# Attention, ELU feed-forward and routed experts in one kernel: a tile's scores beside its neighbour's values, independent table scatters, early expert count from 14 tiles

## Chip, core and metric

The kernel runs on one core of a Trainium2 chip. The metric is the device time of one execution in microseconds (us). Engines are named as the profile names them: PE is TensorE (PEld its weight loads), DVE is VectorE, ACT is ScalarE, POOL is GpSimd, SP is SyncE, which issues most DMAs. Each engine works through its own instructions strictly in the order in which they stand, and waits on semaphores.

## What is computed

Three stages follow each other, on 4 x 576 = 2,304 tokens of width 512 (8 heads of 64):

```python
# 1. attention, causal, window of 64 tokens, float32
scores = where(0 <= pos_i - pos_j < 64, q @ k.T / 8, -1e9)
x = softmax(scores) @ v                      # (2304, 512)
# 2. feed-forward, weights float64: w_in (512, 2048), w_out (2048, 512)
h = x @ w_in
y = where(h > 0, h, exp(min(h, 0)) - 1) @ w_out
# 3. one expert of 8 per token, w1 (8, 512, 1024), w2 (8, 1024, 512)
logits = y @ w_gate + modality_bias[modality_id]     # modality_id is 0 or 1
e = argmax(logits);  gate = softmax(logits)[e]
out = gate * (relu(y @ w1[e]) @ w2[e])
```

With the reference's inputs the bias decides: all tokens fall to two experts, one for each modality.

## The kernel before

**Tiles and units.** The tokens are 18 tiles of 128, or 9 groups of 256. Attention goes by units: unit n = 2t + qd is four heads (qd) of tile t. Each unit is a chain of pieces: `ld`/`lv` load k, q and v (SP); `1p` transposes k and q (PE, 4 matmuls, `p_t`), `1e` copies them out of PSUM; `2p` makes the scores (`p_s`: contraction over 64, output over 64 rows, so the array is split in 64x64 tiles); `2d` adds the mask and takes the maximum (DVE), `2x` the exponential (ACT), `2n` the reciprocal (DVE), `2m` the normalisation (POOL); `3p` transposes the weights (PE, `p_a`), `3a` copies them (`PA`); `4p` multiplies by v (`p_o`: the array split in 128x64 tiles); `4a` and `4d` copy the result as a high and a low part (`xh`, `xl`).

**Feed-forward.** Every product is three float32r products of high and low parts. `f1(g,s)` is 24 matmuls of 256 columns for group g and 256 of the 2,048 inner columns (`h`), `f2(g,s)` 12 matmuls of 512 columns into `y`. Between them stand ACT (`fx`, `fe`, `fh`), DVE (`fm`) and, for the low part, POOL (`fl`, L571) or DVE. The float64 weights are turned into two float32r halves in 32 half-tiles during groups 0 and 1 (`wa` ACT, `wb` DVE, `wc`, `wd`: `wd` on DVE or POOL by the table `LE`).

**Routing.** After a group's `y` the gate takes 8 dot products per tile (`g1`, DVE), the choice (`g2d`), a rank by a matmul with a triangle (`g3p`, PE, `p_rk`; `g3d`, DVE), and `g3s` (POOL, L650), an indirect DMA that writes each token's row of a table `tab` in DRAM, sorted by expert. After 16 of the 18 tiles a first count (`ep` PE, `ed` DVE) finds the expert that has the most tokens, so that its weights can be loaded (`el`, SP) and its first three stages (EA = 3) of 256 tokens can begin: `xa` (SP) reads the table, `xb` (POOL, L879) gathers the rows of y, `xp` transposes them, `e1`/`e2` are the products with 24 and 12 matmuls each. The final count (`rp`, `rd`, `r2`) sets the stages 3 to 8.

**What sets the order.** `program()` lists the pieces with an engine, a cost, a rank, the pieces they need and the buffers they take and free. `plan()` goes through time with these costs and writes each engine's order; the kernel is built in that order. Tables of numbers (ranks such as `G1R`, `RDR`, and ranges such as `LE`, `VIA`, `E1D`, which say on which engine a copy runs) steer it. Up to a planned time of 40 us, PE's planned waits are filled with matmuls on the identity (`fill`).

Of the kernel before, what the change touches and what calls it, by code (L numbers as in the profile page):

```python
# [81 lines left out]
def fused(ctx, tc, q, k, v, w_in, w_out, mod, w_gate, mbias, w1, w2, out):  # L82
# [11 lines left out]
    EA = 3  # L94
# [7 lines left out]
    G1R = 91.22  # L102
    RDR = -290.43
    R2R = -989.45
    EXR = -764.4
    XDR = -890.0
    XBL = 6.4
    SGL = 16.34
    SG = 13.52
    FG = 0.3  # L110
    LV = -17.16
    UR = (0.85, 2.04)
    HE = range(28, 32)
    LE = range(0, 15)
    VIA = range(0, 19)
    E1D = range(0, 6)
    A3D = range(0, 1)
    A4D = range(0, 0)
    FXA = (0, 1, 2, 3, 4, 5, 6, 7, 8)
    YX = (1, 2, 6, 7)  # L120
    LG = 19.41
# [25 lines left out]
    ptp = mkpool("pt", 1)  # L147
# [12 lines left out]
    masks = const.tile([128, 3, 2, 128], F32, name="masks")  # L160
# [72 lines left out]
    def load_gate():  # L233
        cut, fill, zero = RT["sg"]
        wg = cut(128, 4, E)
        nc.sync.dma_start(out=wg, in_=w_gate.rearrange("(k p) e -> p k e", p=128))
        RT["wg"] = wg
        bb = cut(128, 2, E)
        nc.sync.dma_start(out=bb, in_=mbias.partition_broadcast(128))
        md = cut(NTILE, 128, 2, dt=I32)  # L240
        nc.sync.dma_start(out=md, in_=mod.bitcast(I32).rearrange("(t p two) -> t p two", p=128, two=2))
        RT["sg"] = cut, bb, md
        nc.sync.dma_start(out=tab.rearrange("(p r) c -> p r c", p=128), in_=fill)
        for r0, n in ((NT - 256, 128), (NT - 128, 128), (NT, 1)):
            nc.sync.dma_start(out=yd[r0:r0 + n, :].rearrange("p (a b) -> p a b", b=64),
                              in_=zero[0:n].rearrange("p (o b) -> p o b", o=1).to_broadcast([n, DM // 64, 64]))
# [116 lines left out]
    def a2p(t, qd):  # L363
        u = U[t, qd]
        p = u["p2"] = [ps.tile([128, 2, 128], F32, tag="ps", name="p_s") for _ in range(2)]
        for i in range(2):
            for b, r in enumerate(HALF):
                for z in range(2):
                    mm(p[z][r, i], KQ[qd][HALF[z], 2 + i, t % 2, r], window(t, qd, z, i, b), start=True, stop=True)
# [42 lines left out]
    def a4p(t, qd):  # L412
        u = U[t, qd]
        PA, va = u.pop("PA"), u.pop("v")
        po = u["p4"] = ps.tile([128, 2, 128], F32, tag="ps", name="p_o")
        for h in range(4):
            i, z = divmod(h, 2)
            for r, b in zip(HALF, range(2)):
                mm(po[HALF[z], i, r], va[:, b, h], PA[:, h, r], start=True, stop=True)

    def x_at(t, qd):
        return (a[:, 2 * qd:2 * qd + 2, 128 * (t % 2):128 * (t % 2) + 128] for a in X[t // 2])

    def a4a(t, qd, eng):
        if t // 2 not in X:
            new_x(t // 2)
        xh, xl = x_at(t, qd)
        put(eng, xh, U[t, qd]["p4"])

    def a4d(t, qd):  # L430
        po = U.pop((t, qd))["p4"]
        xh, xl = x_at(t, qd)
        dve.tensor_tensor(out=xl, in0=po, in1=xh, op=ALU.subtract)  # L433
# [214 lines left out]
    def g3s(t):  # L648
        GT.pop(t)
        pool.indirect_dma_start(out=tab[:, :], out_offset=bass.IndirectOffsetOnAxis(ap=FI.pop(t)[:, 0:1], axis=0),  # L650
                                in_=ent[:, t, :], in_offset=None)
# [17 lines left out]
    def early_p():  # L669
        p = RT["p0"] = ps.tile([1, E], F32, tag="ps", name="p_c0")  # L670
        mm(p, ones[:, 0:1], cnt[NTILE - 3], start=True, stop=True)

    def early_d():
# [13 lines left out]
        e0, b0 = f0[:, 0:1], f0[:, 1:2]  # L687
        lt = sm("lt0", EA - 1)
        for s in range(1, EA):
            dve.tensor_scalar(out=lt[:, s - 1:s], in0=m0[:, 0:1], scalar1=256.0 * (s + 1), scalar2=None, op0=ALU.is_lt)  # L690
# [4 lines left out]
        for s in range(1, EA):  # L695
# [3 lines left out]
            dve.scalar_tensor_tensor(out=b, in0=gap, scalar=lt[:, s - 1:s], in1=b, op0=ALU.mult, op1=ALU.add)  # L699
# [312 lines left out]
    def program():  # L1012
# [6 lines left out]

        units = [(t, qd) for t in range(NTILE) for qd in range(2)]  # L1020
        for n, u in enumerate(units):
            t, qd = u
            back = t > 0
            early = n < NEARLY
            r = n * UR[0] if n < 8 else 8 * UR[0] + (n - 8) * UR[1]
            add(("ld", n), "SP", 2.9 if n == 0 else KQC * len(list(runs(128 * t, 128))), u_kq, *u, rank=n - 20, need={"w": 1} if early else {"ld": 1},
                lat=1.1 if early else 2.4)
            add(("lv", n), "SP", 0.61 * v_loads(t), u_v, *u, rank=n + LV, deps=[("ld", n)], need={} if early else {"v": 1},
                lat=1.0 if early else 2.4)
            w2p = [("2p", n - 2)] if back else []  # L1030
# [16 lines left out]
            add(("4p", n), "PE", 0.78, a4p, *u, rank=r - 1000, deps=[("3a", n), ("lv", n)] + ([("4p", n - 1)] if n % 4 else []),
                need={"ps": 1} if n % 4 else {"ps": 1, "X": 1},
                free={"PA": 1} | ({"w": 1} if early else {"v": 1}), lat=0.25)
            add(("4a", n), e4, 0.29 if e4 == "ACT" else 0.34, a4a, *u, e4, rank=r,  # L1050
                deps=[("4p", n)] + ([("4a", n - 1)] if n % 4 else []))
            add(("4d", n), "DVE", 0.34, a4d, *u, rank=r, deps=[("4a", n)], free={"ps": 1})
# [18 lines left out]
        for g in range(NG):  # L1071
            for s in range(NP):
# [6 lines left out]
                    deps=[("wd", "i", s, 0), ("wd", "i", s, 1)] + [("4d", 4 * g + x) for x in range(4)] + ([("f1", g, s - 1)] if s else [("f1", g - 1 - (g < NG - 1), NP - 1)] if g > 1 else []),  # L1079
# [18 lines left out]
        add(("sg", 0), "SP", 4.0, load_gate, rank=SG - 20, deps=[("sg", 5)], lat=2.5)  # L1098
# [6 lines left out]
        for t in range(NTILE):  # L1105
# [21 lines left out]
        for j in range(8):  # L1127
            add(("el", j), "SP", 1.8, lambda j=j: e_load(RT["v0"], j), rank=j - 600.0, deps=["ed"] + [("xa", s) for s in range(EA)],
# [3 lines left out]
        for s in range(NS):  # L1132
# [42 lines left out]
        caps = {"w": 33, "ps": 4, "h": 2, "y": 1, "P": 2, "v": 3, "ld": 2, "PA": 1, "X": 3, "e": 2, "g": 3,  # L1175
# [56 lines left out]
```

## Time and profile before

| | |
|---|---|
| median of 3 runs | 760.13 us (759.86 to 760.77) |
| profiled execution | 758.43 us, of which the span from first to last instruction is 756.5 us |
| PE busy | 734.6 us, 97% of the span |
| DVE, ACT, POOL busy | 57%, 44%, 27% |
| granted TensorE clock, mean | 0.993 |

A matmul's row shows its whole passage through the array, and matmuls overlap, so a busy PE says little. What a matmul costs is read from the distance of its start to the start of the next one: the timeline (start, duration, engine, line, operation) has both. A row with a releaser in square brackets was preceded by idle time that this releaser ended. [...]

### The profile page before, as it was taken

The page shows a single profiled execution, that of the slowest core. Times are in us where ns is not written, and L with a number is a line of the kernel's source. Part 1 is how long each engine was busy: PE and PEld are TensorE (multiplying, and loading weights), DVE is VectorE, ACT ScalarE, POOL GpSimd, SP SyncE. Part 2 cuts the span into 40 slices and gives each one's busy share as a digit, 9 for nine tenths or more (in the row PEclk, how much of TensorE's full clock was granted, in tenths as well). Part 3 has the DMA queues.
Part 4 walks back from the last instruction along what each step waited for, and adds up shares of the span by engine and source line. Part 5 has one row for each costly group of instructions (what it writes and reads, how often), then busy time and mean ns, then how long its engine had stood idle before and what let it go on. Part 6 is the DMA issues. An engine that isn't in the chain of part 4 may idle for free. (4 is left out here: it accounts for less than half of the span.)

```text
span 756.5 us, 14736 instructions
## 1 busy us (share of the span) xinstructions
PE 734.6 (97%) x5534; PEld 651.0 (86%) x5534; DVE 430.1 (57%) x1311; ACT 332.6 (44%) x799; POOL 201.0 (27%) x192
## 2 busy tenths in 40 slices
PE   8999999999998999999999999998999999999996
PEld 7878988888886988888988989986988999989995
DVE  6999996899393158194186183584983124421210
ACT  5987854674553463455346333334421114311211
POOL 5201434134223223224224223234024112111011
PEclk9999999999999999999999999999999999999999
DMA  8999532431321031220020000007218212000001
GB/s 204 242 238 294 228 119 113 129 81 30 78 56 41 4 98 29 57 72 22 18 75 1 1 29 1 29 1 254 81 29 293 81 46 72 17 29 14 15 29 43
DMA packets 101020, 62.26 MB, mean 82 GB/s; under 512 B 83697, under 2 KB 87939, under 8 KB 100811
## 3 DMA queue, kind: packets, MB, share of 16 engines
q1 hardware_dynamic: 97323, 51.51, 24.2%
q0 software_dynamic: 3616, 9.72, 3.8%
q8 instruction: 45, 0.74, 0.5%
q14 instruction: 36, 0.29, 0.2%
HBM read 51.05 MB, written 10.42 MB: 81 GB/s over the span
## 5 line engine op out<-in xcount | busy, mean ns | idle before, releaser
L515 PE MATMUL h<-xh,whi 128*128 128x256 f32 x576 | 166.2, 289 | 2.4 <-DVE e L560 2.0
L516 PE MATMUL h<-xl,whi 128*128 128x256 f32 x576 | 163.0, 283 | 0.3 <-DVE xl L433 0.3
L517 PE MATMUL h<-xh,wlo 128*128 128x256 f32 x576 | 162.9, 283 | 0.0
L571 POOL TENSOR_TENSOR g<-e,g 128x512 fp32r<-128x512 f32 x53 | 71.5, 1350 | 183.7 <-ACT g L564 183.5
L524 PE MATMUL y<-whi,g 128*128 128x512 f32 x288 | 118.0, 410 | 0.0
L526 PE MATMUL y<-whi,g 128*128 128x512 f32 x288 | 114.2, 396 | 2.5 <-POOL g L571 2.2
L515 PEld LDWEIGHTS h<-xh,whi 128*128 128x128 f32 x576 | 110.1, 191 | 5.6 <-DVE e L560 2.4
L525 PE MATMUL y<-wlo,g 128*128 128x512 f32 x288 | 113.7, 395 | 0.0
L516 PEld LDWEIGHTS h<-xl,whi 128*128 128x128 f32 x576 | 110.3, 191 | 1.7 <-DVE xl L433 0.5
L517 PEld LDWEIGHTS h<-xh,wlo 128*128 128x128 f32 x576 | 110.1, 191 | 0.0
L560 DVE SCALAR_TENSOR_TENSOR e<-e,h 128x512 f32<-128x512 f32 x53 | 36.3, 685 | 101.0 <-ACT e L551 85.4
L545 ACT ACTIVATE e<-h 128x512 f32<-128x512 f32 x72 | 42.8, 594 | 115.8 <-PE h L517 112.9
L515 PE MATMUL h<-xh,ehi 128*128 128x256 f32 x256 | 72.6, 284 | 0.0
L516 PE MATMUL h<-xl,ehi 128*128 128x256 f32 x256 | 72.5, 283 | 0.0
L517 PE MATMUL h<-xh,elo 128*128 128x256 f32 x256 | 72.5, 283 | 0.0
L526 PEld LDWEIGHTS y<-whi,g 128*128 128x128 f32 x288 | 54.5, 189 | 17.1 <-POOL g L571 2.6
L938 DVE SCALAR_TENSOR_TENSOR g<-h,g 128x512 fp32r<-128x512 f32 x32 | 22.0, 689 | 79.5 <-ACT g L933 79.4
L933 ACT ACTIVATE g<-h 128x512 fp32r<-128x512 f32 x32 | 19.1, 596 | 106.1 <-PE h L517 98.7
L524 PEld LDWEIGHTS y<-whi,g 128*128 128x128 f32 x288 | 54.8, 190 | 12.3 <-issue 2.4
L386 ACT ACTIVATE sm<-sm,st 128x128 f32<-128x128 f32 x144 | 56.0, 392 | 19.6 <-DVE st L379 19.5
L525 PEld LDWEIGHTS y<-wlo,g 128*128 128x128 f32 x288 | 54.9, 191 | 9.2
L601 DVE CUSTOM_DVE_ANT_0 lgs<-ysb,wgb 128x512 bf16<-128x512 f32 x80 | 61.4, 768 | 1.9
(214 smaller groups left out, 1437.8 us busy)
## 6 DMA issues: line engine op xcount, KB each, us to landing
raw<-in_moe_w_in_dram SPq DMA_DIRECT2D x16, 512.0 KB, 5.1
raw<-in_moe_w_out_dram SPq DMA_DIRECT2D x16, 512.0 KB, 5.8
wraw<-in_moe_w_dram SPq DMA_DIRECT2D x16, 512.0 KB, 11.7
v<-in_v_dram SPq DMA_DIRECT2D x46, 128.0 KB, 2.9
kq<-in_k_dram SPq DMA_DIRECT2D x30, 128.0 KB, 2.7
kq<-in_q_dram SPq DMA_DIRECT2D x30, 128.0 KB, 3.0
v<-in_v_dram SPq DMA_DIRECT2D x44, 64.0 KB, 3.0
yd<-ysb SPq DMA_DIRECT2D x10, 256.0 KB, 2.7
```

The lines of the kernel that those rows point to most:

```text
L386: act(out=sm[:, h], in_=sm[:, h], func=AF.Exp, bias=st[:, 0, h:h + 1], scale=-1.0, accum_out=st[:, 1, h:h + 1])
L515: mm(hs[c], w[0][:, d, f], xh, start=d == 0, stop=False)
L516: mm(hs[c], w[0][:, d, f], xl, start=False, stop=False)
L517: mm(hs[c], w[1][:, d, f], xh, start=False, stop=d == 3)
L524: mm(y, gh[:, m], w[0][:, c], start=first and c == 0, stop=False)
L525: mm(y, gh[:, m], w[1][:, c], start=False, stop=False)
L526: mm(y, gl[:, m], w[0][:, c], start=False, stop=last and c == 1)
L545: act(out=e, in_=H[g, s], func=AF.Relu, scale=-1.0)
L560: dve.scalar_tensor_tensor(out=h if via_psum(g, s) else e, in0=e, scalar=-1.0, in1=h, op0=ALU.add, op1=ALU.max)
L571: pool.tensor_tensor(out=a[:, 1], in0=e, in1=a[:, 0], op=ALU.subtract)
L601: dve.tensor_tensor_reduce(out=lgs, in0=y, in1=wgb[:, e], scale=1.0, scalar=0.0, op0=ALU.mult, op1=ALU.add, accum_out=GT[t][:, e:e + 1])
L938: dve.scalar_tensor_tensor(out=g[1][:, c], in0=h, scalar=0.0, in1=g[0][:, c], op0=ALU.max, op1=ALU.subtract)
```

## The change

Four things change. From tile 6 on the two units of a tile are taken together: `24` is one PE piece that makes the values of tile t-1 (both units, one PSUM tile) and then the scores of tile t (both units, two PSUM tiles). It has two `PA` buffers where there was one; the mask is bfloat16; `4a` and `4d` handle both units at once. The table scatters are declared independent of each other. The first count is taken after 14 tiles in place of 16 (`EC`); stage 0 too is now dropped if the largest expert has too few tokens, two more tiles of `yd` are zeroed at the start, and the first three gathers need groups up to 6 alone. The tables and some costs have other numbers, so that all orders differ.

```diff
-    EA = 3
+    EA, EC = 3, NTILE - 4
-    LE = range(0, 15)
-    VIA = range(0, 19)
+    LE = range(0, 27)
+    VIA = range(0, 15)
...
-    ptp = mkpool("pt", 1)
+    ptp = mkpool("pt", 2)
-    masks = const.tile([128, 3, 2, 128], F32, name="masks")
+    masks = const.tile([128, 3, 2, 128], BF16, name="masks")
-        for r0, n in ((NT - 256, 128), (NT - 128, 128), (NT, 1)):
+        for r0, n in [(128 * t, 128) for t in range(EC, NTILE)] + [(NT, 1)]:
...
+    def a2p(t, *qds):
+        p = [ps.tile([128, len(qds), 2, 128], F32, tag="ps", name="p_s") for _ in range(2)]
+        for x, qd in enumerate(qds):
+            U[t, qd]["p2"] = [a[:, x] for a in p]
+            for i in range(2):
+                for b, r in enumerate(HALF):
+                    for z in range(2):
+                        mm(p[z][r, x, i], KQ[qd][HALF[z], 2 + i, t % 2, r], window(t, qd, z, i, b),
+                           start=True, stop=True)
+    def a4p(t, *qds):
+        po = PO[t, qds] = ps.tile([128, 2 * len(qds), 128], F32, tag="ps", name="p_o")
+        for x, qd in enumerate(qds):
+            u = U.pop((t, qd))
+            PA, va = u["PA"], u["v"]
+            for h in range(4):
+                i, z = divmod(h, 2)
+                for r, b in zip(HALF, range(2)):
+                    mm(po[HALF[z], 2 * x + i, r], va[:, b, h], PA[:, h, r], start=True, stop=True)
+    def a24(t):
+        if t > T0:
+            a4p(t - 1, 0, 1)
+        a2p(t, 0, 1)
...
-        pool.indirect_dma_start(out=tab[:, :], ...)
+        r = pool.indirect_dma_start(out=tab[:, :], ..., bounds_check=PAD - 1, oob_is_err=False)
+        tc.declare_no_dep(r.ins, group="tab", reason="different rows")
+        tc.add_to_no_dep_group("tab", r.ins)
...
-        mm(p, ones[:, 0:1], cnt[NTILE - 3], start=True, stop=True)
+        mm(p, ones[:, 0:1], cnt[EC - 1], start=True, stop=True)
...
+                last = t > T0
+                add(("24", t), "PE", 2.54 if last else 1.23, a24, t, rank=r - 1000,
+                    deps=[("1e", n - 1), ("1e", n)] + ([(x, n - y) for x in ("3a", "lv") for y in (2, 3)] if last else []),
+                    need={"ps": 3 if last else 2, "P": 2} | ({"X": 1} if last and t % 2 else {}),
+                    free={"PA": 2, "v": 2} if last else {}, lat=0.25)
...
-                deps=[("xa", s)] + [("fo", NG - 1 if s >= EA else NG - 2, z) for z in range(2)],
+                deps=[("xa", s)] + [("fo", NG - 1 if s >= EA else EC // 2 - 1, z) for z in range(2)],
```

On PE, before, around the values of unit 16 and the scores of unit 19, each product stands apart, with a transpose (`p_a`) between them:

```order
L631 MATMUL p_rk<-cnt,ones 128x8
L419 MATMUL p_o<-PA,v 64x64 x8
L405 MATMUL p_a<-ident,sm 128x128 x4
L369 MATMUL p_s<-kq_108 64x128 x8
L524 MATMUL y<-whi,g 128x512
```

On PE, in the change, the piece `24` of tile 9 (values of tile 8, scores of tile 9; `kq_107` and `kq_108` are the two units' operands):

```order
L528 MATMUL h<-xh,wlo 128x256
L426 MATMUL p_o<-PA,v 64x64 x16
L372 MATMUL p_s<-kq_107 64x128 x8
L372 MATMUL p_s<-kq_108 64x128 x8
L640 LDWEIGHTS tri
```

Four stretches of split-array products per tile have become one, with one border between the two kinds in it.

On POOL, before, at tiles 4 and 5 of the routing (two scatters, and behind the second one the normalisations `2m` of units 22 and 23; a `DMASW` semaphore is that of an earlier indirect DMA):

```order
L571 TENSOR_TENSOR g<-e,g 128x512 [waits PE_49,Activation_49,Pool_49]
L650 DMA tab<-ent,fi 19840x2 [waits DMASW7_49,DVE_49]
L571 TENSOR_TENSOR g<-e,g 128x512 [waits Activation_49]
L650 DMA tab<-ent,fi 19840x2 [waits DMASW0_49,DVE_49]
L397 TENSOR_TENSOR sm<-sm,st 128x512 [waits DVE_49]
```

On POOL, in the change, at the same two scatters:

```order
L582 TENSOR_TENSOR g<-e,g 128x512 [waits Activation_49]
L662 DMA tab<-ent,fi 19840x2 [waits DVE_49]
L582 TENSOR_TENSOR g<-e,g 128x512 [waits Activation_49]
L662 DMA tab<-ent,fi 19840x2 [waits DVE_49]
L401 TENSOR_TENSOR sm<-sm,st 128x512 [waits PE_49,DVE_49,Activation_49,Pool_49] x2
```

The place is the same, but the second scatter no longer waits for the one before it; later scatters wait for the DMA that used the same semaphore eight indirect DMAs earlier.

On POOL, before, where the first gathers (L879) stand, between the low parts of f2(8,5) and f2(8,6), group 8 being the last one:

```order
L650 DMA tab<-ent,fi 19840x2 [waits DMASW6_49,DVE_49]
L571 TENSOR_TENSOR g<-e,g 128x512 [waits PE_49,Activation_49]
L879 DMA xg<-yd,ix 128x512 [waits DMAHW5_49,DMAHW6_49,DMAHW4_49,DMAHW7_49,DMAHW3_49,DMAHW2_49]
L879 DMA xg<-yd,ix 128x512
L571 TENSOR_TENSOR g<-e,g 128x512 [waits Activation_49]
L879 DMA xg<-yd,ix 128x512 [waits DMAHW0_49]
```

On POOL, in the change, the first gathers stand behind the low part of f2(7,7) and ahead of that of f2(8,0):

```order
L582 TENSOR_TENSOR g<-e,g 128x512 [waits Activation_49] x2
L893 DMA xg<-yd,ix 128x512 [waits DMAHW5_49,DMAHW6_49,DMAHW4_49,DMAHW7_49,DMASW6_49,PE_49]
L893 DMA xg<-yd,ix 128x512 [waits DMASW7_49]
L582 TENSOR_TENSOR g<-e,g 128x512 [waits Activation_49]
L582 TENSOR_TENSOR g<-e,g 128x512 [waits PE_49,Activation_49]
```

They have moved from the end of the last group to its beginning.

## Rows read from the trace of the kernel before

**Rows 1.** Waits of PE: line, releaser, total us, times, longest us
```profile
PE p_a L405 <- POOL sm L397: 2.9, 2, 2.3
PE y L526 <- POOL g L571: 2.2, 1, 2.2
PE h L515 <- DVE e L560: 2.0, 2, 1.1
...
PE p_x L885 <- DMA xg<-yd,ix: 1.3, 1, 1.3
...
PE p_rk L629 <- DVE sc L614: 0.9, 1, 0.9
```
**Rows 2.** Windows: stretch, busy us by engine, granted clock, DMA share, GB/s
```profile
230.00:242.00 12.00, 9.74 (x73) 7.63 (x71) 3.09 (x22) 4.02 (x13) 4.38 (x5) 0.86 0.20 45
519.00:526.00 7.00, 5.23 (x20) 3.91 (x21) 4.01 (x3) 3.93 (x6) 5.74 (x6) 0.76 1.02 359
...
60.00:130.00 70.00, 69.75 (x487) 61.11 (x486) 66.09 (x118) 44.18 (x87) 27.97 (x24) 1.00 0.56 185
```
**Rows 3.** Timeline of PE at 286 us: start, duration, instruction; values alone
```profile
286.23 0.39 PE L526 MATMUL y<-whi,g 128*128 128x512 f32 x1
286.55 0.73 PE L419 MATMUL p_o<-PA,v 128*64 128x64 f32 x16
287.21 0.50 PE L524 MATMUL y<-whi,g 128*128 128x512 f32 x1
287.55 0.39 PE L525 MATMUL y<-wlo,g 128*128 128x512 f32 x1
287.78 0.39 PE L526 MATMUL y<-whi,g 128*128 128x512 f32 x1
```
**Rows 4.** Timeline of PE at 271 us: two units' scores together
```profile
270.78 1.10 PE L369 MATMUL p_s<-kq 64*64 64x128 f32 x32
271.82 0.50 PE L524 MATMUL y<-whi,g 128*128 128x512 f32 x1
```
**Rows 5.** Timeline of PE at 148 us: values, then scores, one unit each
```profile
147.65 0.28 PE L516 MATMUL h<-xl,whi 128*128 128x256 f32 x1
147.77 0.28 PE L517 MATMUL h<-xh,wlo 128*128 128x256 f32 x1
147.98 0.73 PE L419 MATMUL p_o<-PA,v 128*64 128x64 f32 x16
148.64 0.67 PE L369 MATMUL p_s<-kq 64*64 64x128 f32 x16
```
**Rows 6.** Timeline of POOL, 229 to 238 us
```profile
229.09 1.00 POOL L650 DMA_INDIRECT tab<-ent,fi  x1 [0.15 <-DVE lg L610]
230.89 1.27 POOL L571 TENSOR_TENSOR g<-e,g 128x512 fp32r<-128x512 f32 x1 [0.80 <-ACT g L564]
235.26 0.98 POOL L650 DMA_INDIRECT tab<-ent,fi  x1 [3.10 <-PE p_o L419]
236.27 2.04 POOL L397 TENSOR_TENSOR sm<-sm,st 128x512 f32<-128x512 f32 x2
```
**Rows 7.** Timeline of DVE at 231 us: the second scatter's indices
```profile
230.98 0.15 DVE L646 CAST fi<-f 128x1 int32<-128x1 f32 x1
```
**Rows 8.** Timeline of DVE at 505 us: the first count begins
```profile
505.45 0.15 DVE L678 COPY arena<-p_c 1x8 f32<-1x8 f32 x1 [0.90 <-PE p_c L671]
```
**Rows 9.** Timeline of POOL, 515 to 519 us
```profile
515.91 0.99 POOL L879 DMA_INDIRECT xg<-yd,ix  x1 [8.11 <-DMA ix<-tab]
...
518.18 1.27 POOL L571 TENSOR_TENSOR g<-e,g 128x512 fp32r<-128x512 f32 x1
```
**Rows 10.** Timeline of ACT at 511 us: high part of f2(8,6)
```profile
510.89 0.63 ACT L564 ACTIVATE g<-e 128x512 fp32r<-128x512 f32 x1 [1.06 <-DVE e L560]
```
**Rows 11.** All scatters (L650): ns min/median/max, first and last start
```profile
L650 POOL DMA_INDIRECT tab<-ent,fi x18: 961/1005/1467, 153.7 to 557.1; - x18
```
**Rows 12.** Low halves of the weights (L492) on DVE, in the same form
```profile
L492 DVE TENSOR_TENSOR wlo<-wf,whi x15: 674/680/1530, 24.4 to 73.5; 128x512 fp32r<-128x512 f32 x15
```

More of the change, by code (lines that the diff above doesn't have):

```diff
@@ L101, in fused @@
     KQC = 1.25
[L102 to L106, printed above, removed]
+    G1R = 50.38
+    RDR = -826.38
+    R2R = -501.44
+    EXR = -622.1
+    XDR = -853.02
     XBL = 6.4
-    SGL = 16.34
-    SG = 13.52
+    SGL = -4.53
+    SG = 20.7
     FG = 0.3
-    LV = -17.16
-    UR = (0.85, 2.04)
-    HE = range(28, 32)
-    LE = range(0, 15)
-    VIA = range(0, 19)
-    E1D = range(0, 6)
-    A3D = range(0, 1)
[L118 to L121, printed above, removed]
+    LV = -16.26
+    UR = (0.86, 0.83)
+    HE = range(24, 32)
+    LE = range(0, 27)
+    VIA = range(0, 15)
+    E1D = range(0, 3)
+    A3D = range(0, 1)
+    A4D = range(0, 4)
+    FXA = (0, 1, 2, 3, 4, 6, 7, 8)
+    YX = (1, 6, 7)
+    LG = 11.18
+    T0 = 6
     NEARLY = 2
@@ L360, in window @@
         return a[:, 1:3] if t % 2 else a[:, 0:4:3]
[L363 to L369, printed above, removed]
+    def a2p(t, *qds):
[7 more added lines that the diff above has]
+                           start=True, stop=True)
     def a2d(t, qd, i):
@@ L410, in a3a, with x_at, a4a, a4d @@
         put(eng, PA, u.pop("p3"))
[L412 to L424, printed above, removed]
+    PO = {}
+    def a4p(t, *qds):
[11 more added lines that the diff above has]
+        a2p(t, 0, 1)
+    def x_at(t, qds):
+        return (a[:, 2 * qds[0]:2 * qds[-1] + 2, 128 * (t % 2):128 * (t % 2) + 128] for a in X[t // 2])
+    def a4a(t, qds, eng):
         if t // 2 not in X:
             new_x(t // 2)
[L427 to L433, printed above, removed]
+        xh, xl = x_at(t, qds)
+        put(eng, xh, PO[t, qds])
+    def a4d(t, qds):
+        xh, xl = x_at(t, qds)
+        dve.tensor_tensor(out=xl, in0=PO.pop((t, qds)), in1=xh, op=ALU.subtract)
     X = {}
@@ L649, in g3s @@
         GT.pop(t)
[L650 to L651 removed]
+        r = pool.indirect_dma_start(out=tab[:, :], out_offset=bass.IndirectOffsetOnAxis(ap=FI.pop(t)[:, 0:1], axis=0),
+                                    in_=ent[:, t, :], in_offset=None, bounds_check=PAD - 1, oob_is_err=False)
+        tc.declare_no_dep(r.ins, group="tab", reason="different rows")
+        tc.add_to_no_dep_group("tab", r.ins)
     SPE = mybir.EngineType.SP
@@ L686, in early_d @@
         f0 = sm("f0", 1 + EA)
[L687 to L690, printed above, removed]
+        e0, b0 = f0[:, 0:1], sm("b00", 1)
+        lt = sm("lt0", EA)
+        for s in range(EA):
+            dve.tensor_scalar(out=lt[:, s:s + 1], in0=m0[:, 0:1], scalar1=256.0 * (s + 1), scalar2=None, op0=ALU.is_lt)
         dve.tensor_reduce(out=d, in_=lt, axis=AX.X, op=ALU.add)
@@ L694, in early_d @@
         gap = sm("gap0", 1)
-        for s in range(1, EA):
+        for s in range(EA):
             b = f0[:, 1 + s:2 + s]
@@ L698, in early_d @@
             dve.tensor_scalar(out=gap, in0=b, scalar1=-1.0, scalar2=float(PAD), op0=ALU.mult, op1=ALU.add)
-            dve.scalar_tensor_tensor(out=b, in0=gap, scalar=lt[:, s - 1:s], in1=b, op0=ALU.mult, op1=ALU.add)
+            dve.scalar_tensor_tensor(out=b, in0=gap, scalar=lt[:, s:s + 1], in1=b, op0=ALU.mult, op1=ALU.add)
         i0 = sm("i0", 1 + EA, dt=I32)
@@ L1018, in add, with P2 @@
             P.append((name, eng, cost, lat, (fn, args), list(deps), rank, need or {}, free or {}))
+        def P2(n):
+            return ("24", n // 2) if n // 2 >= T0 else ("2p", n)
         units = [(t, qd) for t in range(NTILE) for qd in range(2)]
@@ L1029, in program @@
                 lat=1.0 if early else 2.4)
-            w2p = [("2p", n - 2)] if back else []
+            double = t >= T0
+            w2p = [P2(n - 2)] if back else []
             room = [("f1", n // 4 - 3, NP - 1)] if n >= 12 else []
-            add(("1p", n), "PE", 0.55, a1p, *u, rank=r - 1000, deps=[("ld", n)] + w2p + room,
+            add(("1p", n), "PE", 0.44, a1p, *u, rank=r - 1000, deps=[("ld", n)] + w2p + room,
                 need={"ps": 1}, free={} if early else {"ld": 1}, lat=0.25)
@@ L1036, in program @@
             add(("1e", n), e, 0.49 if e == "ACT" else 0.6, a1e, *u, e, rank=r, deps=[("1p", n)] + w2p, free={"ps": 1})
-            add(("2p", n), "PE", 0.7, a2p, *u, rank=r - 1000, deps=[("1e", n)], need={"ps": 2, "P": 1}, lat=0.25)
+            if not double:
+                add(("2p", n), "PE", 0.79, a2p, *u, rank=r - 1000, deps=[("1e", n)], need={"ps": 2, "P": 1}, lat=0.25)
+            elif qd:
+                last = t > T0
[3 more added lines that the diff above has]
+                    free={"PA": 2, "v": 2} if last else {}, lat=0.25)
             for i in range(2):
-                add(("2d", n, i), "DVE", 0.53, a2d, *u, i, rank=r, deps=[("2p", n) if i == 0 else ("2d", n, 0)],
-                    free={"ps": 2} if i else {})
+                add(("2d", n, i), "DVE", 0.53, a2d, *u, i, rank=r,
+                    deps=[("2d", n, 0)] if i else [P2(n)] + ([("2d", n - 1, 1)] if double and qd else []),
+                    free={"ps": 2} if i and (qd or not double) else {})
                 add(("2x", n, i), "ACT", 0.77, a2x, *u, i, rank=r, deps=[("2d", n, i)])
@@ L1043, in program @@
             add(("2m", n), "POOL", 1.05, a2m, *u, rank=r, deps=[("2n", n)], need=L, free=L)
-            add(("3p", n), "PE", 0.5, a3p, *u, rank=r - 1000, deps=[("2m", n)], need={"ps": 1, "PA": 1}, free={"P": 1}, lat=0.25)
+            add(("3p", n), "PE", 0.44, a3p, *u, rank=r - 1000, deps=[("2m", n)], need={"ps": 1, "PA": 1}, free={"P": 1}, lat=0.25)
             e3, e4 = ("DVE" if n in a else "ACT" for a in (A3D, A4D))
             add(("3a", n), e3, 0.49 if e3 == "ACT" else 0.6, a3a, *u, e3, rank=r, deps=[("3p", n)], free={"ps": 1})
[L1047 to L1052, printed above, removed]
+            if not double:
+                add(("4p", n), "PE", 0.86, a4p, *u, rank=r - 1000, deps=[("3a", n), ("lv", n)] + ([("4p", n - 1)] if n % 4 else []),
+                    need={"ps": 1} if n % 4 else {"ps": 1, "X": 1},
+                    free={"PA": 1} | ({"w": 1} if early else {"v": 1}), lat=0.25)
+                add(("4a", n), e4, 0.29 if e4 == "ACT" else 0.34, a4a, t, (qd,), e4, rank=r,
+                    deps=[("4p", n)] + ([("4a", n - 1)] if n % 4 else []))
+                add(("4d", n), "DVE", 0.34, a4d, t, (qd,), rank=r, deps=[("4a", n)], free={"ps": 1})
+            elif qd:
+                if t == NTILE - 1:
+                    add(("4p", n), "PE", 1.55, a4p, t, 0, 1, rank=r - 1000, deps=[(x, n - y) for x in ("3a", "lv") for y in (0, 1)],
+                        need={"ps": 1} if t % 2 else {"ps": 1, "X": 1}, free={"PA": 2, "v": 2}, lat=0.25)
+                add(("4a", n), "ACT", 0.5, a4a, t, (0, 1), "ACT", rank=r,
+                    deps=[("4p", n) if t == NTILE - 1 else ("24", t + 1)] + ([("4a", n - 2)] if t % 2 else []))
+                add(("4d", n), "DVE", 0.6, a4d, t, (0, 1), rank=r, deps=[("4a", n)], free={"ps": 1})
         add("setup", "POOL", 4.0, lambda: None, rank=-9999.0)
@@ L1078, in program @@
                 add(("f1",) + k, "PE", 2.89, f1p, *k, rank=r + 1.5,
-                    deps=[("wd", "i", s, 0), ("wd", "i", s, 1)] + [("4d", 4 * g + x) for x in range(4)] + ([("f1", g, s - 1)] if s else [("f1", g - 1 - (g < NG - 1), NP - 1)] if g > 1 else []),
+                    deps=[("wd", "i", s, 0), ("wd", "i", s, 1)] + [("4d", 4 * g + x) for x in ((1, 3) if 2 * g >= T0 else range(4))] + ([("f1", g, s - 1)] if s else [("f1", g - 1 - (g < NG - 1), NP - 1)] if g > 1 else []),
                     need={"h": 1}, free=({"X": 1} if s == NP - 1 else {}) | ({"w": 2} if g == NG - 1 else {}), lat=0.22)
@@ L1117, in program @@
             add(("g3d", t), "DVE", 0.6, g3d, t, rank=r, deps=[("g3p", t)], free={"ps": 1})
-            add(("g3s", t), "POOL", 1.04, g3s, t, rank=r, deps=[("g3d", t), ("g2b", t)], free={"gs": 1}, lat=2.5)
+            add(("g3s", t), "POOL", 1.3, g3s, t, rank=r, deps=[("g3d", t), ("g2b", t)], free={"gs": 1}, lat=2.5)
         last = NTILE - 1
-        add("iota", "POOL", 0.6, iotas, rank=-700.0, deps=[("g3s", last - 6)], need={"w": 1}, lat=0.5)
-        add("ep", "PE", 0.1, early_p, rank=-2000.0, deps=[("g3d", last - 2)], need={"ps": 1}, lat=0.22)
+        add("iota", "POOL", 0.6, iotas, rank=-700.0, deps=[("g3s", EC - 4)], need={"w": 1}, lat=0.5)
+        add("ep", "PE", 0.1, early_p, rank=-2000.0, deps=[("g3d", EC - 1)], need={"ps": 1}, lat=0.22)
         add("ed", "DVE", 2.6, early_d, rank=-2000.0, deps=["ep", "iota"], free={"ps": 1}, lat=0.5)
@@ L1127, in program @@
         for j in range(8):
-            add(("el", j), "SP", 1.8, lambda j=j: e_load(RT["v0"], j), rank=j - 600.0, deps=["ed"] + [("xa", s) for s in range(EA)],
+            add(("el", j), "SP", 1.6, lambda j=j: e_load(RT["v0"], j), rank=j - 600.0, deps=["ed"] + [("xa", s) for s in range(EA)],
                 need={"w": 1}, lat=2.2)
@@ L1135, in program @@
             wide = s == WIDE
-            add(("xa", s), "SP", 0.3, xl_a, s, rank=k - 650, deps=["ed"] if s < EA else ["rd"], need={"ix": 1}, lat=2.2)
-            add(("xb", s), "POOL", 1.04 * n, xl_b, s, rank=k - 650,
-                deps=[("xa", s)] + [("fo", NG - 1 if s >= EA else NG - 2, z) for z in range(2)],
+            add(("xa", s), "SP", 3.6 if s == 0 else 0.62 if s < EA else 1.1, xl_a, s, rank=k - 650, deps=["ed"] if s < EA else ["rd"], need={"ix": 1}, lat=2.2)
+            add(("xb", s), "POOL", 1.28 * n, xl_b, s, rank=k - 650,
+                deps=[("xa", s)] + [("fo", NG - 1 if s >= EA else EC // 2 - 1, z) for z in range(2)],
                 need={"w": n // 2 + n % 2}, lat=XBL if s < EA else 5.0)
@@ L1163, in program @@
                     need={"w": 1}, free={"y": 1} if t == 1 else {"ps": 1} if t == 2 else {})
-                add(("es", s, t), "POOL", 1.04, es, s, t, rank=k - 800, deps=[("eo", s, t)],
+                add(("es", s, t), "POOL", 1.32, es, s, t, rank=k - 800, deps=[("eo", s, t)],
                     free={"w": 1} | ({"ix": 1} if t == n - 1 else {}))
```

4 lines of the change are left out of this document (2 added, 2 removed).

## The prediction

> **What bounds the kernel now.** I read the page's busy times first: PE is busy nearly all the time (from 60 to 130 us 69.75 of 70 us [rows 2]), so the other engines can matter in one way, by making PE wait at a place. Then the waits of PE, of which only a few are long, each named by its releaser [rows 1]. Then the windows, which show that two of these places cost more than their wait: around 230 to 242 us the granted clock is 0.86, around 519 to 526 us it is 0.76, and elsewhere 1.00 [rows 2]. [...] Last the timeline, for what a piece costs on PE. There the reader is to look at starts, not at durations: a `y` matmul follows the one before by 0.23 us (287.55 to 287.78), an `h` matmul by 0.12 us [rows 3, 5]. So f1 takes 24 x 0.12 = 2.9 us and f2 12 x 0.23 = 2.8 us, and PE is a queue of such blocks with attention pieces in between. The time is this queue plus PE's waits, and the change touches both.
>
> **Term 1, fewer stretches of split-array products.** A unit's values alone: PE comes to them 0.09 us late (286.23 to 286.55 is 0.32, not 0.23), stays 0.66 us until the next `y` starts, and that `y` is 0.11 us slow (287.21 to 287.55): 0.86 us [rows 3]. Scores of two units in one stretch stay 1.04 us (270.78 to 271.82) [rows 4], and with the same 0.09 and 0.11 make 1.24 us. The rows' durations for two units and for one, 1.10 and 0.67, differ by 0.43 [rows 4, 5], so a second unit costs 0.43 and one unit alone 0.81. Where scores follow values at once, the values still hold PE 0.66 us (147.98 to 148.64) [rows 5]: the border between the two kinds costs as much as leaving, and only one slow return and one late entry, 0.20 us, are saved.
>
> The doubled piece is then 0.86 + 0.81 - 0.20, and two second units. For the scores that is 0.43. For the values no row shows a second unit; it is between 0.43 (as the scores) and 0.66 (nothing overlaps), and I take 0.50, near the score's row. Sum: 2.4 us. From tile 6 on, the order before has 16 units of scores alone, 4 pairs, and 24 units of values alone, one border among them: 16 x 0.81 + 4 x 1.24 + 24 x 0.86 - 0.2 = 38.4 us. The order after has one pair of scores (tile 6), 11 doubled pieces, and the values of tile 17: 1.24 + 11 x 2.4 + 1.36 = 29.0 us. PE is the queue that is never empty there, so nothing hides this: minus 9.4 us. I take 9.0, since a transpose behind values returns a little faster than a `y`. Bounds: 0, if the second units overlap with nothing and enter and leave as before, to 10.2, if a values' second unit costs 0.43.
>
> **Term 2, independent scatters.** The place is 229 to 238 us. The second scatter's index is ready at 231.1 [rows 7] and POOL is free at 232.2 (230.89 + 1.27), but the scatter starts at 235.26, 6.2 us after the one before began [rows 6]. The row names PE as releaser; those products have nothing to do with the scatter, and its order row names the earlier DMA's semaphore. Behind it stand two normalisations, and behind these PE's transposes, which waited up to 2.3 us [rows 1]; and the clock fell: (1 - 0.86) x 12 = 1.7 us [rows 2]. Without the wait the scatter runs from 232.2 to 233.2 [rows 11] and the first normalisation, half of 2.04, ends at 234.2, before PE has finished the values that it began at 234.4. So the whole goes: minus 4.0 us, bounds 0 (another wait takes over) to 4.6 (all 2.9 us of this wait).
>
> First the row: the 18 scatters took POOL 961 to 1467 ns, median 1005, beside a DVE at work [rows 11]. [...]
>
> **Term 3, the earlier count.** Before, the count starts at 505.45 [rows 8], the gathers at 515.91, and the low part behind them on POOL at 518.18 [rows 9], though its input was there at 511.5 [rows 10]. PE waited 2.2 us for it and then 1.3 us for the gathered rows [rows 1], and lost clock: (1 - 0.76) x 7 = 1.7 us, part of it inside the second wait, so I count 1.1 (0.4 to 1.7) [rows 2]. After, between the count on PE and f2(8,0), whose low part stands behind the first gathers, the order has 9 blocks, 5 x 2.9 + 4 x 2.8 = 25.7 us. The chain is 10.5 us to the gathers, 2.3 for two of them, 1.3 for the low part [rows 8, 9]: 14.1 us. That leaves 11 us of cover. The transposes of stage 0 come seven blocks later still. What is late next is the first split of the expert's weights: on DVE it stands ahead of `fm` of f1(8,1); its buffer comes free with f1(8,0), and f2(8,1), which would wait in the end, is six blocks or 17 us later. Minus 4.6 us, bounds 0 to 5.2. The additional small DVE operations of the count lie inside this cover.
>
> **Term 4, other waits.** The largest others (`h` for DVE, 2.0 us in two waits, and `p_rk` for DVE, 0.9) are places where a gate's run of DVE work stood ahead of a copy [rows 1]. All these places are laid out anew. In the order after I find no attention piece on PE with less than one f1 block (2.9 us) between it and what it needs, but the gate can collide elsewhere. Of 2.9 us I count 2 as gone; bounds plus 4 (as much again as term 2 removes) to minus 2.9.
>
> **Term 5, the beginning.** From 60 to 130 us DVE is busy 66.1 of 70 us with PE at 69.8 [rows 2]: both nearly full. The change brings 12 low halves from POOL to DVE, at 0.68 us each [rows 12] up to 8.2 us, and four high halves; it takes three copies of transposes and a few low parts away. Eight more fills and two more zeroing DMAs come in. What hides this is DVE's 4 us and its lead over PE. I take plus 2, bounds minus 2 to plus 8.
>
> The bfloat16 mask, the joined `4a`/`4d` and the second `PA` buffer change the work of engines that have room, and no row shows them otherwise: nothing, within 1 us either way.
>
> **Sum.** -9.0 - 4.0 - 4.6 - 2 + 2 = -17.6. The profiled execution took 758.4 us, 756.5 of them span; 758.4 - 17.6 = 740.8. The median of the runs is 1.7 us above the profiled one, so 742.5, rounded to 742.
>
> **Rivals.** *The doubled pieces save nothing* (term 1 is 0): each product could need its own entry. Against it stand the pairs of scores [rows 4], which cost 1.24 where two alone would cost 1.62; for it, that no row has two units of values. 742 + 9 = 751. *DVE becomes the bound from 60 to 130 us*: term 5 is plus 8. For it its 66 of 70 us, against it that POOL's halves end on time before and that the half tiles run ahead. 748. *All goes well*, with term 1 at -10.2, term 3 at -5.2, term 4 at -2.9 and term 5 at 0: 738. *The doubled piece couples too much*, the case for slower: it waits for the last of two units' copies, two units' weights and two loads of v, with three v buffers. Each of the 11 stretches could wait as long as the longest of PE's waits, 2.3 us [rows 1]: 25 us, so 767. It decides from 1.6 us a stretch, where 17.6 us are used up. Against it: at least one f1 block of 2.9 us stands between the last transpose and the doubled piece, and the copy between them is one ACT instruction of some 0.6 us. *The early count is too early*: if the largest expert had fewer than 768 tokens in 14 tiles, a stage would run empty and another be added, 4 x (2.9 + 2.8) = 23 us, 765. The reference's inputs give it 899 of 1,792, so this needs other inputs.
>
> **Chances.** Forecast 0.70, with 736 to 747 as its own range; nothing saved by doubling 0.10; DVE the bound 0.08; all well 0.05; coupling 0.06; empty stage 0.01. The range 734 to 753 takes in all but the last two, and the bounds of terms 1, 4 and 5 one at a time. A change within 0.2%, 1.5 us, can't be told from none; that could only come from a partial coupling, 0.02. Faster 0.91, slower 0.07.
>
> **What would show it.** In the profile after: doubled pieces of 2.3 to 2.5 us between neighbours' starts (term 1); no POOL row L662 that starts over 1 us after its index and POOL are ready, and no half clock before 500 us (term 2); no PE wait for `g` or `xg` near the end of group 8, and no half clock there (term 3); PE waits after 60 us of under 3 us in all (term 4); PE idle for less than 1 us between 60 and 130 us (term 5). I am wrong if doubled pieces wait for `PA` or `v`, or if PE waits for `wlo` or `e` between 50 and 130 us.

## Result and profile after

The changed kernel takes 738.65 us (median of 4 runs, 737.92 to 739.65) where before takes 760.0 in the same comparison: a ratio of 0.9722, 95% interval 0.9702 to 0.9742, so 21 us less. The forecast was 742 us. The profiled execution took 738.16 us, 736.4 of them span, 20.1 less than the span before.

The waits of PE, all of them (line, releaser, total us, times, longest us; answers to [rows 1]):

```profile
PE p_a L409 <- POOL sm L401: 1.7, 2, 1.0
PE fill L1219 <- POOL ident L188: 1.5, 1, 1.5
PE p_o L426 <- DVE wlo L503: 0.8, 1, 0.8
PE p_o L426 <- DMA v<-in_v_dram: 0.8, 1, 0.8
PE p_rk L640 <- DVE sc L625: 0.6, 1, 0.6
PE h L526 <- DVE g L580: 0.4, 1, 0.4
PE p_o L426 <- issue: 0.2, 1, 0.2
PE p_t L345 <- DMA kq<-in_q_dram: 0.2, 1, 0.2
PE p_s L372 <- DVE kq L351: 0.2, 1, 0.2
```

The two long waits of before are gone, and no wait for `xg`, for POOL's `g` or for `e` is left. The windows (columns as in [rows 2]) say the same of the clock, as a share of full speed: it is 1.00 in all three. PE does not idle in the first, around the place that lost clock near 237 us; in the second, around the end of group 8, it idles 0.61 us, all of it the wait of `p_rk` above.

```profile
226.00:238.00 12.00, 12.00 (x81) 10.97 (x81) 4.39 (x21) 7.00 (x24) 5.40 (x5) 1.00 0.18 30
470.00:500.00 30.00, 29.39 (x184) 26.15 (x183) 27.96 (x67) 16.63 (x27) 12.86 (x10) 1.00 0.59 158
60.00:130.00 70.00, 68.62 (x463) 61.71 (x462) 65.80 (x133) 42.78 (x81) 7.82 (x11) 1.00 0.55 168
```

The other signs that were named are there too: no scatter (L662) starts more than 0.6 us after its index and POOL are ready, there is no half clock between 7 and 733 us (granted 1.00; before had 0.50 from 238 to 241 and from 521 to 524 us), and PE's waits behind 60 us come to 2.0 us.

A doubled piece in PE's timeline (start, duration; answers to [rows 3 to 5]):

```profile
148.98 0.28 PE L528 MATMUL h<-xh,wlo 128*128 128x256 f32 x1
149.19 1.20 PE L426 MATMUL p_o<-PA,v 128*64 128x64 f32 x32
150.32 1.10 PE L372 MATMUL p_s<-kq 64*64 64x128 f32 x32
151.35 0.50 PE L535 MATMUL y<-whi,g 128*128 128x512 f32 x1
151.69 0.40 PE L536 MATMUL y<-wlo,g 128*128 128x512 f32 x1
```

Entry 0.09 late, 1.13 for the values, 1.03 for the scores, return 0.11 late: 2.36 us, as for eight of the 11 pieces; three have the rank's products behind them, 2.41.

**Where the 20.1 us of span went.** Both kernels can be cut at one piece, the start of f1(2,0), at 137.17 us before and 138.84 us after. The window up to there, of before:

```profile
0.00:137.17 137.17, 131.52 (x1154) 113.53 (x1154) 120.76 (x312) 95.39 (x243) 45.60 (x56) 1.00 0.72 207
```

and of after:

```profile
0.00:138.84 138.84, 132.75 (x1170) 116.26 (x1170) 118.92 (x330) 95.03 (x240) 27.84 (x44) 1.00 0.72 202
```

PE has done the same 1,154 products in both, and after 16 fills more. So the beginning costs 1.7 us more, although the scores of units 12 and 13, one stretch in place of two, save 0.4 in it: 2.1 without them. Behind the cut the span falls from 619.3 to 597.6, by 21.8.

What PE lost at a wait is read from starts: the time between two matmuls, less the usual distances of what stands between them. The dearest place of before:

```profile
516.91 0.39 PE L525 MATMUL y<-wlo,g 128*128 128x512 f32 x1
519.50 0.50 PE L526 MATMUL y<-whi,g 128*128 128x512 f32 x1 [2.21 <-POOL g L571]
...
525.54 0.48 PE L524 MATMUL y<-whi,g 128*128 128x512 f32 x1
```

Between the first and the last of these starts lie 8.6 us, for eleven steps of `y` (0.23 us each) and eight transposes that take 0.8 us where nothing waits: 3.3 us, so 5.3 are lost, waits and half clock together. In the same way before lost 3.9 at 237 us, 4.5 at four other waits (222, 229, 339 and 404 us) and 0.3 at 345 us, where scores start late without a wait that has a row; after loses 0.8, at 487 us. That is 13.2 of the 21.8 us.

The stretches between feed-forward products are summed in the same way, each with its late entry and its slow return and without the losses just named. Behind the cut they take 67.4 us before and 58.8 after: 8.6 us, which is the rest.

### The profile page after: what moved, and what is told of

Read it like the earlier page. It is cut to its first block, busy times and chain, and to the rows that moved or that the text cites. A ratio compares the mean times of both kernels' runs of the same rounds, so it can differ in the third digit from the quotient of the medians.

```text
span 736.4 us, 14731 instructions
## 1 busy us (share of the span) xinstructions
PE 722.5 (98%) x5550; PEld 649.7 (88%) x5550; DVE 429.7 (58%) x1324; ACT 326.1 (44%) x774; POOL 192.7 (26%) x184
## 5 line engine op out<-in xcount | busy, mean ns | idle before, releaser
L582 POOL TENSOR_TENSOR g<-e,g 128x512 fp32r<-128x512 f32 x57 | 80.0, 1403 | 190.8 <-ACT g L575 167.1
L535 PE MATMUL y<-whi,g 128*128 128x512 f32 x288 | 116.0, 403 | 0.0
L537 PE MATMUL y<-whi,g 128*128 128x512 f32 x288 | 112.5, 391 | 0.0
L571 DVE SCALAR_TENSOR_TENSOR e<-e,h 128x512 f32<-128x512 f32 x57 | 39.1, 686 | 85.6 <-ACT e L562 72.0
L612 DVE CUSTOM_DVE_ANT_0 lgs<-ysb,wgb 128x512 bf16<-128x512 f32 x96 | 79.5, 828 | 2.5 <-ACT ysb L599 0.6
L556 ACT ACTIVATE e<-h 128x512 f32<-128x512 f32 x64 | 38.1, 595 | 94.0 <-PE h L528 93.6
```

What stands on the lines that cost most here:

```text
L535: mm(y, gh[:, m], w[0][:, c], start=first and c == 0, stop=False)
L537: mm(y, gl[:, m], w[0][:, c], start=False, stop=last and c == 1)
L556: act(out=e, in_=H[g, s], func=AF.Relu, scale=-1.0)
L571: dve.scalar_tensor_tensor(out=h if via_psum(g, s) else e, in0=e, scalar=-1.0, in1=h, op0=ALU.add, op1=ALU.max)
L582: pool.tensor_tensor(out=a[:, 1], in0=e, in1=a[:, 0], op=ALU.subtract)
L612: dve.tensor_tensor_reduce(out=lgs, in0=y, in1=wgb[:, e], scale=1.0, scalar=0.0, op0=ALU.mult, op1=ALU.add, accum_out=GT[t][:, e:e + 1])
```

## Experiments

Ratios are to the kernel before, and differences to it are worked out from the ratio; differences to the changed kernel are between medians, which come from different comparisons and can be off by about 1 us.

**Independent scatters alone (b_scatter)**, in before:

```diff
-        pool.indirect_dma_start(out=tab[:, :], ...)
+        r = pool.indirect_dma_start(out=tab[:, :], ..., bounds_check=PAD - 1, oob_is_err=False)
+        tc.declare_no_dep(r.ins, group="tab", reason="different rows")
+        tc.add_to_no_dep_group("tab", r.ins)
```

> The kernel before with one edit: the table scatters are declared independent of each other; every engine's order is that of before. Theory (term 2): the second scatter of tiles 4 and 5 starts within 1 us of its index and of POOL, PE's wait of 2.3 us for the normalisation near 237 us and the half clock behind it go: 4 us less, about 756. [...]

755.9 us, ratio 0.9939 (0.9912 to 0.9966): 4.6 us less, 2.6 to 6.7. The timeline of POOL at the place of [rows 6], and then of PE (in brackets the idle time before, and what ended it):

```profile
231.95 1.27 POOL L571 TENSOR_TENSOR g<-e,g 128x512 fp32r<-128x512 f32 x1 [0.79 <-ACT g L564]
233.38 0.99 POOL L650 DMA_INDIRECT tab<-ent,fi  x1 [0.16 <-DVE st L379]
234.40 1.05 POOL L397 TENSOR_TENSOR sm<-sm,st 128x512 f32<-128x512 f32 x1
...
235.45 0.73 PE L419 MATMUL p_o<-PA,v 128*64 128x64 f32 x16
236.11 0.66 PE L405 MATMUL p_a<-ident,sm 128*128 128x128 f32 x4
```

The scatter starts 0.16 us behind the low part and takes 0.99 us; the transposes follow the values with no wait. The theory holds. The 18 scatters of this execution took POOL 966 to 1468 ns, median 1006, as in [rows 11]. Near 520 us this execution waited longer for gathered rows than before (3.4 us) and shorter for `g` (1.0 us), which nothing in the edit asks for.

**Early count alone (b_count)**, in before:

```diff
-    EA = 3
+    EA, EC = 3, NTILE - 4
...
-        mm(p, ones[:, 0:1], cnt[NTILE - 3], start=True, stop=True)
+        mm(p, ones[:, 0:1], cnt[EC - 1], start=True, stop=True)
```

> The kernel before with the early count alone: after 14 tiles, with the two more zeroed tiles, stage 0 under a condition, and the first gathers needing groups up to 6. Scatters and split-array pieces are those of before; pieces near the end of routing move in the order. Theory (term 3): no wait of PE for g or xg near 520 us and no half clock there: 4.6 us less, about 755.5. Rival: the gathers, which now stand ahead of two scatters and low parts on POOL in groups 7 and 8, make other pieces late; then under 2 us are gained, over 758.

755.31 us, ratio 0.9941 (0.9920 to 0.9962): 4.5 us less. PE has no wait from 503 to 750 us, and around the first transposes of gathered rows, at 508.5 us, the steps of `y` stay at 0.23 to 0.24 us; the wait of 2.5 us for the normalisation stays (here at 240 us), and the mean granted clock is 0.995, not the 0.998 of the changed kernel. The theory holds.

**Both (b_both)**, the two edits together:

> The kernel before with both the independent scatters and the early count, without doubled pieces and with its own tables. Theory (terms 2 and 3 add, since their places lie 280 us apart): the sum of the two alone, 4.6 + 4.5 = 9.1 us less, about 751. Rival (one of them takes over what the other leaves, as the gathers came later in the run with independent scatters alone): 753 to 756.

752.7 us, ratio 0.9889 (0.9872 to 0.9905): 8.4 us less, 7.2 to 9.7. The sum of the two, 9.1, lies inside: they add.

**No doubled pieces (a_single)**, in the changed kernel:

```diff
-    T0 = 6
+    T0 = NTILE
```

> The changed kernel without doubled pieces: each unit's values and scores are pieces of their own for all tiles; scatters and early count stay as changed, and the order is planned anew. Theory (term 1): 9 us slower than the changed kernel, about 748; its PE has again some 45 stretches of split-array products after 140 us where the changed kernel has 13. Rival (doubled pieces save little, and the gain came from places laid out anew): under 4 us slower, below 743.

747.19 us, ratio 0.9825 (0.9796 to 0.9854): 8.5 us slower than the changed kernel. On the ratios it is 7.8. Behind the cut its stretches between feed-forward products sum to 68.0 us of PE, the changed kernel's to 59.6, which is 8.5 too; but 0.6 of this is a wait for `sc` that the changed kernel does not have, its only additional wait behind 60 us. So some 7.9 us hang on the doubled pieces. The theory holds, a little under its 9.

**Two more borders in each doubled piece (a_borders)**:

```diff
-            a4p(t - 1, 0, 1)
-        a2p(t, 0, 1)
+        for x in range(2):   # values of unit x of tile t-1, then scores of unit x of tile t
+            ...
```

> The changed kernel with the products inside each doubled piece in another sequence: values of one unit, its scores, values of the other, its scores. The same products, waits and place in the order, but three borders between the two kinds of split in place of one, in 11 pieces. Theory (a border costs about what a second stretch's entry costs, 0.81 - 0.43 = 0.38 us less the 0.20 saved, so 0.2 to 0.4 us each): 22 borders, 4 to 9 us slower, 743 to 748, and a doubled piece of 2.8 to 3.1 us. Rival (only the border with unsplit products costs): doubled piece still 2.36 us, same time within 1 us.

741.86 us, ratio 0.9755 (0.9725 to 0.9785): 3.2 us slower, its span 4.0 longer. The piece in PE's timeline:

```profile
149.78 0.73 PE L439 MATMUL p_o<-PA,v 128*64 128x64 f32 x16
150.45 0.67 PE L444 MATMUL p_s<-kq 64*64 64x128 f32 x16
151.04 0.73 PE L439 MATMUL p_o<-PA,v 128*64 128x64 f32 x16
151.71 0.67 PE L444 MATMUL p_s<-kq 64*64 64x128 f32 x16
152.31 0.50 PE L549 MATMUL y<-whi,g 128*128 128x512 f32 x1
```

From the first value to `y` 2.53 us where the changed kernel has 2.16: 0.37 for two borders, the same in all 11 pieces, and 11 times 0.37 is 4.1 us. The rival (such a border is free) falls by these rows; the times alone would not do, since the intervals of the two ratios overlap a little. The expectation was somewhat dear: 2.8 to 3.1 us a piece where it is 2.73, and 4 us at least in the time where it is 3.2.

**Dependent scatters in the changed kernel (a_serial)**: the two added lines on the group `tab` taken out again.

> The changed kernel with one edit: the scatters depend on each other again, as before the change; every engine's order stays. Theory (term 2 as a cost that the place sets): with the order laid out anew, a normalisation still stands behind the second scatter of tiles 4 and 5, so PE waits there again, 2 to 4 us slower, 741 to 743. Rival (the new order alone has taken the place away): within 1 us of the changed kernel.

737.55 us, ratio 0.9695 (0.9671 to 0.9719): not slower; the intervals overlap. The rival was right. The timeline of POOL, with PE's transposes as the last row, in a_serial:

```profile
230.05 0.99 POOL L662 DMA_INDIRECT tab<-ent,fi  x1 [2.61 <-DVE st L396]
231.07 1.05 POOL L401 TENSOR_TENSOR sm<-sm,st 128x512 f32<-128x512 f32 x1
232.54 1.04 POOL L401 TENSOR_TENSOR sm<-sm,st 128x512 f32<-128x512 f32 x1 [0.42 <-ACT e L562]
...
233.66 1.03 PE L409 MATMUL p_a<-ident,sm 128*128 128x128 f32 x8
```

The same in the changed kernel:

```profile
227.55 0.99 POOL L662 DMA_INDIRECT tab<-ent,fi  x1 [0.50 <-DVE fi L657]
229.60 1.03 POOL L401 TENSOR_TENSOR sm<-sm,st 128x512 f32<-128x512 f32 x1 [1.07 <-DVE st L396]
231.12 1.04 POOL L401 TENSOR_TENSOR sm<-sm,st 128x512 f32<-128x512 f32 x1 [0.48 <-DVE st L396]
...
233.25 1.03 PE L409 MATMUL p_a<-ident,sm 128*128 128x128 f32 x8
```

The scatter waits again, and POOL ends 1.4 us later (233.58 against 232.16), but PE's transposes of both units now stand behind a whole f2 and come at 233.66. The new order alone is enough at this place: it leaves 1.1 us of room with independent scatters and 0.1 without.

**First count after 16 tiles in the changed kernel (a_count16)**:

```diff
-    EA, EC = 3, NTILE - 4
+    EA, EC = 3, NTILE - 2
```

> The changed kernel with the first count after 16 tiles as before, the rest as changed. Theory (term 3): a wait for g or xg of 2 to 3.5 us and half clock come back near the end of group 8: 4.6 us slower, about 743. Rival (the new order of group 8 has room for it): under 2 us slower.

754.6 us, ratio 0.9924 (0.9894 to 0.9954): 16 us slower, far beyond what theory and rival had. Its longest waits of PE:

```profile
PE p_rk L640 <- DVE sc L625: 4.1, 1, 4.1
PE h L526 <- ACT xh L912: 3.4, 1, 3.4
PE h L528 <- DVE elo L868: 2.4, 1, 2.4
```

All three stand between 511 and 532 us, with clocks of 0.66, 0.88 and 0.61 in 10 us each from 510 us. The order is planned anew here and mixes the gate's last products with the first stage, and the expected waits for `g` and `xg` are not among the long ones (`xg` 0.7 us, `g` 0.4). So this says nothing clean of the count; b_count does.

**The changed code with the tables of before (a_oldtables)**, such as:

```diff
-    G1R = 50.38
+    G1R = 91.22
...
-    LE = range(0, 27)
+    LE = range(0, 15)
```

> The changed kernel's code with the number tables of before (which engine makes which halves and copies, and the ranks of the gate, the attention and the splits). Theory (terms 4 and 5: the tables take away some 2 us of waits elsewhere, and the beginning costs 2 us more for DVE's extra halves): within 3 us of the changed kernel, as the two cancel. Rival (the tables are where the gain beyond the forecast comes from): 3 to 10 us slower, with waits of PE for DVE or POOL between 50 and 500 us.

756.93 us, ratio 0.9950 (0.9931 to 0.9969): 18 us slower than the changed kernel, and only 3.8 better than before. Its longest waits of PE in sum between 60 and 500 us:

```profile
PE p_rk L640 <- DVE sc L625: 6.1, 7, 1.1
PE y L535 <- ACT g L575: 3.6, 2, 2.1
PE p_o L426 <- ACT PA L349: 1.4, 1, 1.4
```

With 0.96 of the clock from 60 to 140 us. The rival holds, and past its upper end.

**The code of before with the changed tables (b_newtables)**, the opposite edit:

> The kernel before with the changed kernel's tables of numbers, its code being that of before. Theory (the tables fit one order of pieces, and their worth comes from being laid for it): 5 to 20 us slower, 765 to 780, with PE waiting for halves of weights or for the gate. Rival (the tables are better in themselves, which would make them the source of the gain): 3 to 15 us faster, 745 to 757.

787.01 us, ratio 1.0325 (1.0297 to 1.0353): 25 us slower, beyond the theory's 5 to 20, and the rival falls. New tables alone lose 25 us, new code alone gains 4, both gain 21: the tables are worth nothing in themselves, they fit one order.

**Doubled pieces from tile 4 on (a_t4)**:

```diff
-    T0 = 6
+    T0 = 4
```

> The changed kernel with the doubled pieces from tile 4 on in place of tile 6. Theory (term 1): two more tiles trade some 3.2 us of separate stretches for one of 2.36, so 0.8 us each, 1.5 us faster, about 737. Rival (in groups 1 and 2, where DVE and ACT have no room, the coupled units come late): 1 to 4 us slower, with PE waits for PA, sm or kq before 140 us.

751.07 us, ratio 0.9868 (0.9843 to 0.9892): 12 us slower than the changed kernel. The rival was right in sign, not in size, nor in what PE waits for. Its window around 110 us:

```profile
100.00:120.00 20.00, 17.04 (x93) 15.02 (x93) 19.00 (x38) 8.01 (x14) 1.61 (x1) 0.83 0.06 22
```

and its longest waits of PE from 100 to 160 us:

```profile
PE h L526 <- DVE g L580: 2.5, 1, 2.5
PE y L536 <- POOL wlo L503: 2.5, 2, 1.5
PE y L535 <- ACT g L575: 1.3, 1, 1.3
```

DVE is busy for 19.0 of 20 us, and PE waits for it and for weight halves in feed-forward products. None of its 13 doubled pieces waits. The order is planned anew here with tables laid for doubled pieces from tile 6 on, and a_oldtables shows that tables which do not fit can cost 18 us; so it stays open whether the doubled pieces or the tables make these waits.

**Without the late fills (a_fill33)**:

```diff
-    FILL = 40.0
+    FILL = 33.0
```

> The changed kernel without the fills planned after 33 us; 28 fill matmuls, 3.4 us of PE's queue between 35 and 40 us, go, all else stays. Theory (the fills stand where PE would wait anyway: the scores behind the last 20 need a copy of kq that ACT ends at 39.8 us): same time within 1 us. Rival (the 2 us that the beginning costs more are the 16 fill matmuls that the changed order has beyond the 64 of before): 2 us or more faster, about 736.

739.24 us, ratio 0.9709 (0.9693 to 0.9725): the same. In place of the fills PE waits 1.5 us for `xl` and 1.9 us for `kq`, and the clock falls; the window from 37 us:

```profile
37.00:45.00 8.00, 5.13 (x28) 3.89 (x29) 7.96 (x25) 6.86 (x24) 1.31 (x1) 0.68 0.97 268
```

DVE is busy for 7.96 of these 8 us. The execution shown is the longest of the four (741.20). The fills cost nothing there; they stand where PE would wait for DVE and ACT.

## Why the prediction was right

The time lies inside the forecast's own range, 736 to 747. The first term came out as argued. The third and the fourth held by their mechanism and were taken too small, both past their bounds. The second and the fifth came right in size, but not, or only in part, for the reason given.

- *Fewer stretches of split-array products*, -9.0 forecast, -9.0 measured (8.6 behind the cut, 0.4 ahead of it). The doubled piece was put at 2.4 us and is 2.36, since a second unit of values costs 0.46 (two alone take 1.32), not 0.50: 0.4 us more over 11 pieces. As much went the other way. Values and transposes in one stretch take 1.24 us in before, apart they take 0.86 and 0.45; behind the cut before has 13 such joint stretches and after none, 0.9 us where I had allowed 0.4. a_single confirms the size by another way, 7.8 to 8.5; a_borders that a border costs by itself.
- *Independent scatters*, -4.0 forecast, -3.9 in the trace and -4.6 by b_scatter. But in the changed kernel a_serial shows that the new order would have taken this wait away without them. I read the place as unchanged because the instructions on POOL were the same; what had changed was PE, where the transposes behind them stand later. The size was right, but that it belongs to the scatters was not: in the changed kernel either edit suffices, and the time there would have been the same without the one I named.
- *The earlier count*, -4.6 forecast, -5.3 in the trace, just past the bound of 5.2, and -4.5 (2.9 to 6.1) by b_count. Behind the waits of 2.2 and 1.3 us I counted 1.1 for the clock; with the slow step behind each wait it was 1.8. The cover is longer than argued. The count starts on DVE, the first gather on POOL and the first transpose of gathered rows on PE at these times in the changed kernel:

```profile
444.40 0.15 DVE L692 COPY arena<-p_c 1x8 f32<-1x8 f32 x1 [0.90 <-PE p_c L685]
...
458.82 0.99 POOL L893 DMA_INDIRECT xg<-yd,ix  x1 [1.60 <-PE h L528]
...
490.39 0.38 PE L899 MATMUL p_x<-ident,xg 128*128 128x128 f32 x2
```

The gathers come 14.4 us behind the count, not 10.5, and 32 us ahead of their use.
- *Other waits*, -2 forecast, -4.0 measured, past my bound of -2.9: I had counted `h` and `p_rk` alone and left out a wait of 0.7 us of `p_s` for DVE near 404 us, and each wait costs PE 0.1 to 0.3 us more than its idle time. What I did not see is how much hangs on this term: a_oldtables is 18.3 us worse, so with the tables of before this term and the next would come to some +17 together, not -1.9. The bound of +4 held only for the order that I had read.
- *The beginning*, +2 forecast, +2.1 measured, and that the size fits is luck: the reason given does not show. DVE did not get more to do up to the cut, 118.92 us against 120.76, although 27 low halves ran on it where 15 did [rows 12]; what it lost made up for that. It and ACT bound 35 to 45 us, as a_fill33 shows (busy for 7.96 and 6.86 of the 8 us from 37 us), and the 16 more fill matmuls (I had read eight) stand for longer waits there. Why these are longer stays open. PE idles 1.38 us between 60 and 130 us, not under 1.

So -9.0 - 3.9 - 5.3 - 4.0 + 2.1 = -20.1, the change of the span, where -17.6 was forecast. Of the rivals, *the doubled pieces save nothing* is excluded by a_single, *DVE the bound from 60 to 130 us* by the window above, *coupling* by PE's waits: none of the 11 pieces waits, nor does one of the 13 in a_t4.

## What to carry to other kernels

Price a piece that splits the array by its borders: count the stretches and the borders in them first; a second unit in a stretch costs about half of the first here (0.46 us after 0.86 for values, 0.43 after 0.81 for scores). Where an engine is the queue that is never empty, a wait can be removed at either end, by an earlier input or a later use, so test each edit both added to the old kernel and taken from the new one. Tables that steer an order belong to one program: a change judged with the old tables shows a fifth of its worth here.

## What was not expected of the hardware

A border between 128x64 and 64x64 products inside a stretch costs 0.18 us each time (0.37 for two, in a_borders), a little less than I had expected. And in a_fill33 the mean granted clock was 0.68 from 37 to 45 us, around two waits of 1.5 and 1.9 us, with no cost to the whole that the times show (739.24 us against 738.65); DVE was busy for 7.96 of these 8 us and ACT for 6.86.
